# Column halves for the first batch's transform products and three idle products

## The chip, the cores and the metric

The kernel runs on one core of one Trainium2 chip. The metric is the device time of one execution in microseconds; lower is better.

## The reference

Two blocks follow each other. The first is an mLSTM cell over 4 batches, 8 heads, 768 tokens and 40 features a head: a recurrence with a running maximum m for stability.

```
m_new = max(f + m, i);  f_stab = exp(f + m - m_new);  i_stab = exp(i - m_new)
C = f_stab * C + i_stab * outer(v, k);   n = f_stab * n + i_stab * k
y[t] = sigmoid(o) * (C q) / max(|n . q|, 1)
```

Its output, rearranged to x of shape (4, 768, 320), goes into an FNet block: the real part of a two-dimensional Fourier transform over tokens and features, a normalisation, and two dense layers.

```
mixed = real(fft(fft(x, axis=1), axis=2));   u = x + mixed
un = (u - mean(u)) / sqrt(var(u) + 1e-6)
out = u + relu(un @ w_ch1) @ w_ch2           # 320 -> 1280 -> 320
```

## The kernel before

The recurrence is cut into six chunks of 128 tokens a batch. Each chunk needs many small products on TensorE, which all go through the helper `product` (line L587): scores `ps`, outputs `ph` (in the first batch `hb`), and contributions to the state. For batches 1 to 3 they use quadrants of the 128x128 array, so that several run side by side. The maxima of the first batch are spread by `spread_max` (L228, L233).

The Fourier transform uses symmetry. `mix_fold` (L892 to L905) folds tokens and features into sums and differences (`fe`, `fe_odd`). `mix_seq` and `mix_tail` transform over tokens. For the first batch both call `mix_products`, which writes 386 columns (`NK`) for each of three pairs of chunks p, in the order p = 2, 1, 0, and for both parts i (cosine and sine); only part 0 of p = 1 is done otherwise, as two products of 193 columns each (L967, L968, every second column). The results `pz` (128 features) and `pzt` (the last ones, in 64-column tiles, two side by side) are copied by ScalarE to `Z` and `Zt` (L881). `mix_feat` (L1004) then transforms over features: three products of 321 columns for each p into `pu`, and two of 161 columns (`own`) at p = 1. VectorE adds `pu` to x (`mix_add`, L1020) and takes the statistics (L1027, L1028); ScalarE centres (`uc`, L1042), TensorE turns (`put`, L1053), and the dense layers follow: `mlp_in` and the products around it (L1134, L1151, L1217), and the second layer (L1289, L1346). In batches 1 to 3 the transform runs in `mix_products_again` (L958).

While this runs, VectorE and ScalarE also unpack the dense weights from 64-bit words (`Piece`: L465, L467, L473, L480, L483, L487).

`idle_products` (L143) multiplies a tile of zeros into a bank that nobody reads. It is called with three products at the start, before the first gates arrive, and with two more after the last chunk of the first batch.

The order of the work is written out by hand: `at(slot, phase, function)` puts every step into a plan, and `run` issues the steps in order of slot and phase. So every engine executes its instructions in the order in which the plan issued them. Loads and stores are issued from SyncE's queue.

Of the kernel before, what the change touches and what calls it, by code (L numbers as in the profile page):

```python
# [19 lines left out]
L = 128  # L20
# [10 lines left out]
TG = NT // 2  # L31
# [8 lines left out]
NK = HALF + 2  # L40
# [17 lines left out]
def kernel(  # L58
# [15 lines left out]
    nc = tc.nc  # L74
# [19 lines left out]
    def bank(name, shape, n=None):  # L94

        return ps_m.tile(shape, FP, name=name, tag=f"pm{next(turn) if n is None else n}")
# [8 lines left out]
    ds_sb = const.tile([L, TG, 2, NK], FP, name="ds_sb")  # L105
    dd_sb = const.tile([L, 4, DM + 1], FP, name="dd_sb")
    fe = const.tile([L, TG, 2 * PAD], FP, name="fe")
# [29 lines left out]
    EVAC, FILL, MAIN, FILL_PE = range(4)  # L137


    def idle_products(n, rest, at_=None):  # L140
        pw = bank("pi", [L, 2 * L], at_)
        for i in range(n):
            nc.tensor.matmul(pw, rest[:, 0:L], rest, start=True, stop=True, skip_group_check=True)  # L143


    def gates(gp):
# [3 lines left out]
        rest = gp.tile([L, 2 * L], FP, name="rest")  # L150
# [16 lines left out]
        nc.vector.memset(ebias, -896.0 * 2.0**23)  # L167
        nc.gpsimd.memset(qk_bufs[0][:, 0], 0.0)
        nc.scalar.activation(out=warm[:, 0:1], in_=rest[:, 0:1], func=AF.Exp)
        idle_products(3, rest)  # L170
        mlstm_load(0, 0)
        make_identity(nc, ident)
        nc.gpsimd.memset(later_r, 0.0)
# [248 lines left out]
        for c in range(2, NT):  # L422
            for h0 in (0, NP):
                at(3 * c - 1, FILL_PE + 2, spread_max, 0, c, h0)
        at(17, FILL_PE + 2.7, idle_products, 2, rest, 3)
        at(2, FILL + 0.5, columns_late)
        at(2, FILL + 0.6, clear, *gb_bufs)
# [86 lines left out]
    def mlstm_load(b, c):  # L514
        k = chunks[b, c] = Chunk()
        i = b * NT + c
        k.qk = qk_bufs[i % NQ]
        k.C = [states[(c + n if b == 0 else b * NS + 2 * c + n) % len(states)] for n in range(3)]
        for hip in range(2):
            nc.sync.dma_start(out=k.qk[hip * 64:hip * 64 + D], in_=qkT[b, c, hip])  # L520
        kvt = kvp.tile([L, H * (D + D1) + LH - D], FP, name="kvt", tag="kvt")
        nc.sync.dma_start(out=kvt, in_=kv[b, c])
        k.v, k.k = kvt, kvt[:, H * D1:]
        k.v1 = k.v[:, 0:H * D1].rearrange("p (h d) -> p h d", d=D1)
# [394 lines left out]
    def mix_seq(b, p, parts):  # L919


        k = mixes.setdefault(b, Mix())
        if p == TG - 1:
            k.pz = getattr(k, "pz", []) + [bank("pz", [L, NK], MIX[b - 1]["z"][i] if b > 0 else (3, 0)[i]) for i in parts]
        for i in parts:
            if b == 0:
                mix_products(p, k.pz[i], i, slice(0, L))
            else:
                for product in mix_products_again(k, k.pz[i], i, slice(0, L)):
                    product()  # L930

    def mix_tail(b, p):

        k = mixes[b]
        if p == TG - 1:
            k.pzt = bank("pzt", [L, NK], MIX[b - 1]["zt"]) if b > 0 else first_heads_ps[:, 0, 0:NK]
        halves = [k.pzt[i * 64:(i + 1) * 64] for i in range(2)]
        if b == 0:
            for i in range(2):
                mix_products(p, halves[i], i, slice(L, PAD))  # L940
        else:

            a, z = (mix_products_again(k, halves[i], i, slice(L, PAD)) for i in range(2))
            for product in (a[0], z[0], a[1], z[1], a[2], z[2], a[3]):
                product()
# [17 lines left out]
    def mix_products(p, out, i, m):  # L963
        fm = slice(i * PAD + m.start, i * PAD + m.stop)
        kw = dict(stop=(p == 0), skip_group_check=True)
        if i == 0 and p == TG - 2:
            nc.tensor.matmul(out[:, 0:NK:2], fe[:, p, fm], ds_sb[:, p, 0, 0:NK:2], start=False, **kw)  # L967
            nc.tensor.matmul(out[:, 1:NK:2], fe_odd[:, m], ds_sb[:, p, 0, 1:NK:2], start=False, **kw)  # L968
        else:
            nc.tensor.matmul(out, fe[:, p, fm], ds_sb[:, p, i], start=(p == TG - 1), **kw)  # L970

    def mix_seq_out(b, i):
        k = mixes[b]
# [9 lines left out]
    def mix_feat(b, p, part=slice(None)):  # L983

        k = mixes[b]
        m = slice(COL[p], COL[p] + L)
        if part.start in (None, 0):  # L990
            k.pu[p] = bank("pu", [L, DM + 1 + NC], MIX[b - 1]["u"][p] if b > 0 else None)
        pu = k.pu[p]
        if b == 0:
            products = ((pu[:, 0:DM + 1], k.Z[:, 0, m], dd_sb[:, 0]), (pu[:, 0:DM + 1], k.Z[:, 1, m], dd_sb[:, 1]),
                        (pu[:, 0:DM + 1], k.Zt[:, m], dd_sb[:, 2]))
        else:
            products = ((pu[:, 0:NC], k.Z[:, 0, m], dd_sb[:, 0, 0:NC]), (pu[:, NC:DM], k.Z[:, 1, m], dd_sb[:, 1, 1:HALF_D]),
                        (pu[:, 0:DM], k.Zt[:, m], dd_sb[:, 3, 0:DM]))
        if p == TG - 2:
            own = first_heads_ps[:, 1, 0:NC] if b == 0 else pu[:, DM + 1:]  # L1000
            z, zt = (t[:, LAST:LAST + 1].to_broadcast([L, L]) for t in (k.Z[:, 0], k.Zt))
            products += ((own, z, dd_sb[:, 0, 0:NC]), (own, zt, dd_sb[:, 3, 0:NC]))
        for i, (o, z, t) in list(enumerate(products))[part]:
            nc.tensor.matmul(o, z, t, start=(i == 0 or b == 0 and i == 3), stop=(i in (2, 4)), skip_group_check=True)  # L1004

    def mix_add(b, c):

# [74 lines left out]
    def plan_mix(b, s0, x_done, s_feat, s_add, s_turn):  # L1082
# [20 lines left out]
        for p in range(TG):  # L1103
            for i in range(3) if b == 0 and p == TG - 1 else ():
                at(s_feat[p] + i, FILL_PE + 5.1, mix_feat, b, p, slice(i, i + 1))
            if b == 0 and p == TG - 2:
                at(s_feat[p], FILL_PE + 4.06, mix_feat, b, p, slice(0, 3))
                at(s_feat[p] + 1, FILL_PE + 4.95, mix_feat, b, p, slice(3, 5))
            elif b == 0 and p == 0:
                at(s_feat[p], FILL_PE + 4, mix_feat, b, p, slice(0, 2))  # L1110
                at(s_feat[p], FILL_PE + 4.04, mix_feat, b, p, slice(2, 3))
            elif b > 0 or p < TG - 1:
                at(s_feat[p], FILL_PE + 4, mix_feat, b, p)
# [316 lines left out]
    hid.update({(0, r): mlp_p.tile([L, NFF // 2 * TG * L], FP, name=f"h0{r}") for r in range(2)})  # L1430
    gates_pool = ExitStack()
    gates(gates_pool.enter_context(tc.tile_pool(name="gates", bufs=1)))


# [212 lines left out]
```

## Time and profile before

| | |
|---|---|
| median of 3 runs | 383.57 us (379.48 to 384.47) |
| the profiled execution | 382.09 us |
| its span, first to last instruction | 380.2 us |
| TensorE passes, busy | 373.3 us, 4,602 |
| TensorE weight loads, busy | 278.2 us, 4,602 |
| VectorE busy | 280.8 us |
| ScalarE busy | 171.4 us |
| GpSimd busy | 133.9 us |
| mean granted TensorE clock | 0.999 |

The profile calls TensorE's passes PE, its weight loads PEld, VectorE DVE, ScalarE ACT, GpSimd POOL, and SyncE's queue SPq. Durations of passes are modelled and overlap; how fast they follow each other is read from their start times. An fp32 product stands in the profile as two weight loads and two passes. "issue" as the reason of a wait means that the profile shows nothing that the engine waited for. Queue q8 carries instructions, not data.

### The profile page before, as it was taken

Reading aid. Unit: us, or ns where it says so; the run is one execution under the profiler, and the core shown is the slowest. Engines: PE = TensorE matmul, PEld = TensorE weight load, DVE = VectorE, ACT = ScalarE, POOL = GpSimd, SP = SyncE. Lnnn points to the kernel's source line nnn. Section 1 sums busy time; section 2 is a strip of 40 time slices with the busy share of each in tenths; the row PEclk is TensorE's granted clock in tenths of the full one; section 3 lists DMA queues with packets and bytes.
Section 4 is the critical chain, followed back from the end, with each engine's and each line's share of the span. In section 5 each row is a group of like instructions: output and inputs, shape, how many; then the busy total and the mean of one; then the engine's idle time right before and its main releaser. Section 6 shows DMA issues by size and latency. Waiting matters only on the chain.

```text
span 380.2 us, 11433 instructions
## 1 busy us (share of the span) xinstructions
PE 373.3 (98%) x4602; PEld 278.2 (73%) x4602; DVE 280.8 (74%) x662; ACT 171.4 (45%) x501; POOL 133.9 (35%) x240
## 2 busy tenths in 40 slices
PE   8999999999999999999999999999999999999996
PEld 6887655567677777666578999676488996546996
DVE  7788999999998585787964787987745885245552
ACT  4878757756442114764442153854520233544000
POOL 5568433775686124471501424561300000020000
PEclk9999999999999999999999999999999999999999
DMA  7978565999870428460002737300000001000011
GB/s 195 284 219 287 168 184 148 252 241 265 278 207 29 127 66 238 134 174 26 0 3 62 205 99 195 102 3 3 0 2 34 17 20 36 0 0 2 34 36 34
DMA packets 20500, 41.93 MB, mean 110 GB/s; under 512 B 3256, under 2 KB 9744, under 8 KB 20320
## 3 DMA queue, kind: packets, MB, share of 16 engines
q1 hardware_dynamic: 20448, 41.21, 37.5%
q8 instruction: 36, 0.59, 0.7%
q14 instruction: 16, 0.13, 0.1%
HBM read 37.10 MB, written 4.10 MB: 108 GB/s over the span
## 4 chain that ended last, share of the span: by engine, by line
PE 79%; DVE 9%; ACT 2%; issue 1%; SPq 1%; POOL 1%; DMA 0%; DVEq 0%; ACTq 0%; POOLq 0%
PE po L1346 22%; PE pm L1217 19%; PE po L1289 8%; PE pm L1134 7%; PE ph L587 5%; PE pm L1151 4%; PE ps L587 4%; PE pu L1004 3%; PE pz L958 2%; PE put L1053 2%; PE pzt L958 1%; PE hb L587 1%; DVE e L480 1%; DVE stats L1027 1%; DVE e L465 1%
## 5 line engine op out<-in xcount | busy, mean ns | idle before, releaser
L1295 DVE SCALAR_TENSOR_TENSOR x<-po,rstd,x 128x160 f32<-128x160 f32 (+1 forms) x69 | 27.1, 394 | 36.3 <-PE po L1346 33.0
L1223 DVE TENSOR_TENSOR h<-h,pm 128x384 f32<-128x384 f32 x60 | 30.5, 550 | 24.2 <-PE pm L1217 11.8
L583 POOL TENSOR_SCALAR_AFFINE_SELECT W<-W 64x512 f32<-64x512 f32 x36 | 28.1, 780 | 37.8 <-ACT W L556 28.8
L1217 PE MATMUL pm<-uT,w_sb 128*128 128x384 f32 x90 | 37.3, 503 | 0.1
L556 ACT ACTIVATE W<-W,colT 128x64 f32<-128x64 f32 x144 | 36.6, 336 | 1.6 <-DMA W<-M_d 1.6
L710 POOL TENSOR_TENSOR C<-C,decB 128x164 f32<-128x164 f32 x33 | 18.1, 549 | 49.4 <-DVE C L717 45.9
L1289 PE MATMUL po<-w_sb,h 128*128 128x320 f32 x120 | 33.6, 432 | 0.0
L1134 PE MATMUL pm<-uT,w_sb 64*64 64x384 f32 x320 | 32.0, 496 | 0.0
L1077 POOL TENSOR_TENSOR t<-rstd 128x6 f32<-128x6 f32 x12 | 3.7, 311 | 76.1 <-DVE v L1071 75.6
L568 POOL TENSOR_TENSOR qg<-qk,Gb 128x512 f32<-128x512 f32 x21 | 28.1, 1337 | 4.5 <-DMA Gb<-G_d 4.2
L1289 PEld LDWEIGHTS po<-w_sb,h 128*128 128x128 f32 x120 | 22.5, 190 | 8.9
L1151 PE MATMUL pm<-uT,w_sb 128*128 128x384 f32 x80 | 28.4, 496 | 0.0
L1346 PE MATMUL po<-T,S 128*128 128x160 f32 x180 | 27.8, 301 | 0.2 <-DVE x L1295 0.2
L1346 PEld LDWEIGHTS po<-T,S 128*128 128x128 f32 x180 | 25.4, 190 | 1.3 <-DVE x L1295 0.4
L1346 PE MATMUL po<-w_sb,h 128*128 128x160 f32 x180 | 26.3, 300 | 0.0
L1346 PEld LDWEIGHTS po<-w_sb,h 128*128 128x128 f32 x180 | 25.2, 190 | 1.4 <-DVE x L1295 0.3
L1217 PEld LDWEIGHTS pm<-uT,w_sb 128*128 128x128 f32 x90 | 15.7, 189 | 12.1 <-DVE h L1223 4.1
L1272 ACT ACTIVATE h<-h 128x384 f32<-128x384 f32 x45 | 23.1, 520 | 2.9 <-DVE h L1223 2.9
L1134 PEld LDWEIGHTS pm<-uT,w_sb 64*64 64x64 f32 x320 | 11.1, 132 | 15.5 <-issue 13.4
L574 POOL TENSOR_TENSOR vw<-kvt,colT 128x328 f32<-128x328 f32 x23 | 19.6, 852 | 7.0 <-DVE colT L290 2.7
L1151 PEld LDWEIGHTS pm<-uT,w_sb 128*128 128x128 f32 x80 | 14.3, 190 | 10.1 <-issue 1.2
L587 PE MATMUL ps<-qk 40*64 40x64 f32 (+1 forms) x768 | 19.9, 240 | 0.3 <-DVE C L717 0.3
(255 smaller groups left out, 825.2 us busy)
## 6 DMA issues: line engine op xcount, KB each, us to landing
kvt<-in_kv SPq DMA_DIRECT2D x24, 336.0 KB
qk<-in_qkT SPq DMA_DIRECT2D x48, 160.0 KB
raw<-in_w SPq DMA_DIRECT2D x10, 640.0 KB
W<-M_d SPq DMA_DIRECT2D x36, 128.0 KB
so<-in_o SPq DMA_DIRECT2D x24, 160.0 KB
out<-x SPq DMA_DIRECT2D x23, 160.0 KB
Gb<-G_d SPq DMA_DIRECT2D x42, 80.0 KB
ds_sb<-in_dft_s SPq DMA_DIRECT2D x1, 1158.0 KB
```

Source lines behind the costliest of these rows:

```text
L556: nc.scalar.activation(out=k.W[:, h, :], in_=M, func=AF.Exp, scale=-1.0, bias=colT[:, c, 0, b * H + h:b * H + h + 1])
L568: nc.gpsimd.tensor_tensor(out=k.qg[:, :, t], in0=k.qk[:, 0, :, t], in1=k.Gb[:, :, t], op=OP.mult)
L583: nc.gpsimd.affine_select(out=W, in_=W, compare_op=OP.is_ge, fill=0.0, base=base, pattern=[[0, H], [-1 if back else 1, LH]], channel_multi ...
L587: nc.tensor.matmul(out, w, x, start=start, stop=True, skip_group_check=True)
L1134: nc.tensor.matmul(banks[i][half(cols)], w1_rest(n)[half(i), half(cols)], u[half(i)], start=start, stop=not start, skip_group_check=True)
L1151: nc.tensor.matmul(k.pm[i], w1_block(ch, f // 2 * 2 + i), u[2 * ch], start=(ch == 0 and not ahead), stop=(ch == 1 and (ahead or n in (2, 5 ...
L1217: nc.tensor.matmul(bank, w, u, start=start, stop=True, skip_group_check=True)
L1223: nc.vector.tensor_tensor(out=h, in0=h, in1=bank, op=OP.add)
L1272: nc.scalar.activation(out=h, in_=h, func=AF.Relu, scale=-1.0)
L1289: nc.tensor.matmul(k.po[m], hidden(gr, f)[:, i * L:(i + 1) * L], w2_sb[:, f, :], start=(f == 0), stop=(f == NFF - 1))
L1295: nc.vector.scalar_tensor_tensor(out=u, in0=po, scalar=k.rstd[:, c:c + 1], in1=u, op0=OP.mult, op1=OP.add)
L1346: nc.tensor.matmul(po, a[:, f], w[:, f], start=start and f == 0, stop=f == half - 1, skip_group_check=True)
```

## The change

Three kinds of products of the first batch's stretch are issued as two products over halves of their columns, with the same weights: the first three idle products (256 columns become 128 and 128), the ten products of `mix_products` over 386 columns (193 and 193), and the nine products of `mix_feat` over 321 columns (160 and 161). Each half loads its weights again. The flag that clears a bank stays with the first half alone. The two later idle products, the `own` products and all other batches are as before. What follows in TensorE's program stands 88 instructions later.

```diff
+    def columns_of(n, parts):
+        return [slice(i * n // parts, (i + 1) * n // parts) for i in range(parts)]
+
-    def idle_products(n, rest, at_=None):
+    def idle_products(n, rest, at_=None, halves=1):
         pw = bank("pi", [L, 2 * L], at_)
         for i in range(n):
-            nc.tensor.matmul(pw, rest[:, 0:L], rest, start=True, stop=True, skip_group_check=True)
+            for cols in columns_of(2 * L, halves):
+                nc.tensor.matmul(pw[:, cols], rest[:, 0:L], rest[:, cols], start=True, stop=True, skip_group_check=True)
...
-        idle_products(3, rest)
+        idle_products(3, rest, halves=2)
...
-            nc.tensor.matmul(out, fe[:, p, fm], ds_sb[:, p, i], start=(p == TG - 1), **kw)
+            for cols in columns_of(NK, 2):
+                nc.tensor.matmul(out[:, cols], fe[:, p, fm], ds_sb[:, p, i, cols], start=(p == TG - 1 and cols.start == 0), **kw)
...
-            nc.tensor.matmul(o, z, t, start=(i == 0 or b == 0 and i == 3), stop=(i in (2, 4)), skip_group_check=True)
+            for cols in columns_of(o.shape[1], 2 if b == 0 and i < 3 else 1):
+                nc.tensor.matmul(o[:, cols], z, t[:, cols], start=(cols.start == 0 and (i == 0 or b == 0 and i == 3)),
+                                 stop=(i in (2, 4)), skip_group_check=True)
```

## The prediction

> **What bounds the kernel now.** I read the page's busy times first, then the chain of waits in stretches, then TensorE's own timeline around the products that the change cuts, and last the few places where TensorE stands still although nothing holds it.
>
> ```profile
> PE 373.3 (98%) x4602; PEld 278.2 (73%) x4602; DVE 280.8 (74%) x662; ACT 171.4 (45%) x501; POOL 133.9 (35%) x240
> q8 instruction: 36, 0.59, 0.7%
> PE 79%; DVE 9%; ACT 2%; issue 1%; SPq 1%; POOL 1%; DMA 0%; DVEq 0%; ACTq 0%; POOLq 0%
> ```
>
> TensorE is busy for 98% of the span and carries 79% of the chain that ended last. So any time that the change adds to TensorE's program, or takes from it, moves the end, except where another engine holds the chain. The whole chain can therefore not shrink by much: all of TensorE's idle time together is 380.2 - 373.3 = 6.9 us, and some 3 us of that are the last stores after its last pass at 377.1 us. The chain of waits between 36 and 60 us, where most of the cut products run, shows such a place:
>
> ```profile
> 50.27 1.78 DVE w_sb L487
> ...
> 52.08 0.63 DVE e L465
> 52.71 0.40 DVE m L467
> 53.11 0.41 DVE x L1020
> ```
>
> Here VectorE holds the chain, not TensorE: it unpacks weights (L487, L465, L467) and gets to the first add of the transform (L1020) only then. The timeline has TensorE's last two passes for that add (Zt, line L1004) from 51.37 to 52.18; VectorE takes the result up at 53.04, 0.86 us later. What TensorE loses between 42 and 52 us, up to 0.86 us, costs nothing.
>
> **The price of cutting a product.** Each fp32 product appears as two weight loads and two passes (L143: six passes for three products). The change turns 3 + 10 + 9 = 22 products into 44, which is 22 x 4 = 88 instructions. The total number of columns stays the same, so the cost is what a pass costs beyond its columns.
>
> ```profile
> 45.70 0.51 PE L967 MATMUL pz<-ds_sb,fe 128*128 128x193 f32 x2
> 46.04 0.50 PE L968 MATMUL pz<-ds_sb,fe_odd 128*128 128x193 f32 x2
> ```
>
> Columns are start, time, what and count. Two passes of 193 columns take 46.04 - 45.70 = 0.34 us, 170 ns each from start to start. Successive 386-column passes at L970 start 324 ns apart in the same timeline once the first weights are loaded. Two halves then take 340 ns, 16 ns more. These 193-column passes write every second column, and the new ones write neighbouring columns, so 16 ns is my upper bound; the lower is nothing, since the columns are the same. The ten transform products have 20 passes; in the tail products two 64-column tiles run side by side (L970 on hb starts its passes in pairs, at 48.80 and 48.81), so about 15 lie one behind another (10 of the sequence products and 5 steps of the tail's): 0 to 15 x 16 = 0.24 us. The nine feature products (321 columns, passes 270 ns apart) become 160 and 161 columns, and 161-column passes start 136 ns apart: 2 x 136 - 270 = 2 ns, 18 times, 0.04 us. All but the last two or three of these passes lie under VectorE's chain. I take 0.01 us for what gets through and keep 0.28 us for the case that the cover is gone. The weight loads come double, but a load overlaps the pass before it: in L967's two passes each has its own load and they still start 0.17 us apart.
>
> The first three idle products run slowly: passes of 256 columns start 0.43 us apart, and at L233, just after, passes of 128 columns start 0.21 us apart with a load each. Twelve of 0.21 are as long as six of 0.43. What follows them (L273 at 4.10) waits for the last one; I take 0, with 0.1 us either way.
>
> No wait, transfer or queue entry is added; only the last half of a product carries the signal that the whole carried, so ScalarE's copies of Z start when the second half is done. They lie under the same cover.
>
> **The place in the program.** All that follows stands 88 instructions later. That matters only if a position has a price, and one place in the trace looks like it:
>
> ```profile
> 146.86 0.30 PEld L1004 LDWEIGHTS pu<-dd_sb,Z 128*128 128x128 f32 x2
> 147.70 0.32 PEld L1004 LDWEIGHTS pu<-dd_sb,Z 128*128 128x128 f32 x2 [0.54 <-issue]
> 146.86 0.40 PE L1004 MATMUL pu<-dd_sb,Z 128*128 128x161 f32 x1
> 147.69 0.57 PE L1004 MATMUL pu<-dd_sb,Z 128*128 128x161 f32 x3 [0.43 <-issue]
> ```
>
> The second pass of one product has its weights from 147.16 on (loads at 146.86 and 146.97) and the same inputs as the first, yet it starts at 147.69: 0.53 us in which it waits for no engine and no transfer. I read it as an instruction that had not arrived. The page gives queue q8 36 packets of 0.59 MB, 16 KB each; TensorE has 9,204 loads and passes and 93 semaphore instructions, 258 per packet, so q8 brings TensorE's program in blocks of about 256. Narrow windows of the DMA view put one q8 packet into 144.90 to 145.06 and none into 146.2 to 147.2. If the late pass is the first of a block, the others begin every 256 instructions from it, and the block before began at about 144.75 and ran out 2.4 us later. The shortest stretches of 256 instructions, as they stand now (first two) and 88 instructions on (last three):
>
> ```profile
> 144.75:147.70 2.95, 2.52 (x142) 2.37 (x135) 0.72 (x2) 0.61 (x3) 1.34 (x4) 1.00 0.89 226
> 246.10:248.60 2.50, 2.50 (x131) 2.10 (x127) 1.69 (x4) 2.15 (x9) 1.84 (x3) 1.00 0.01 3
> 231.99:235.77 3.78, 3.78 (x141) 3.73 (x133) 2.45 (x8) 1.83 (x5) 1.78 (x3) 1.00 0.47 142
> 169.60:173.52 3.92, 3.92 (x131) 2.74 (x129) 3.18 (x8) 1.42 (x4) 0.82 (x2) 1.00 0.55 144
> 69.70:74.00 4.30, 4.29 (x142) 2.91 (x135) 4.01 (x7) 3.06 (x9) 3.20 (x5) 1.00 0.89 291
> ```
>
> The first number after the window is its length, the first in brackets counts passes, the last but one is the DMA share. Shifted by 88, no block is used up in less than 3.78 us, while the late one needed 2.95. The first took its delay with the DMA engines 89% busy; the one of 2.50 us, with DMA idle, went without. So I expect the 0.53 us to go. The work after it is TensorE's own (L1053, then L1289 without a gap), so the gain passes on. I take -0.5 us, between 0 (it isn't the block) and -0.53.
>
> **The sum.** The profiled execution took 382.09 us, its span 380.2. -0.53 + 0.01 + 0 gives 381.6. The three runs shown have a median of 383.57 and go from 379.48 to 384.47, so the profiled one lies 1.5 below the median, inside their spread of 5 us. 2% of this kernel is 7.7 us, about what a measurement of it can tell from no change. The forecast is no measurable change, with 381.6 us as the time.
>
> **Rivals.**
>
> (1) *The place has no price.* The 0.53 us is something that the trace does not name, and stays. Against it: nothing else there is late. For it: it is a single case, and the 2.50-us block has no gap. Time: 382.09 + 0.01 = 382.1. The Trainium skill speaks for this rival: Runtime: NRT & Kernel Launch, section "Instruction fetch mechanics", says that blocks of 256 instructions are fetched while the previous one executes, and that instruction fetch is hidden because dispatch is slower than the refill. The 0.53 us at 147.2 disagrees with that as far as one case can.
>
> (2) *A new block comes late: slower than before.* Its place is one of the shortest shifted stretches, in or beside the bursts of small products of L587, with 232.0 and 169.6 first. From the start of a block to its packet took 0.3 us in the late case, but up to 3.7 us elsewhere (the next packet starts between 151.35 and 151.50, its block began at 147.70). The packet took 1.28 us and its use came 1.36 us after, so the next block can be there 2.9 to 6.3 us after the start. It decides from 3.78 us on. At the worst end 6.3 - 3.78 = 2.5 us are lost at that one place: 381.6 + 2.5 = 384.1. For over 2%, all four of the shortest (the fourth lasts 4.69 us) would have to be late at the worst end, 2.5 + 2.4 + 2.0 + 1.6 = 8.5 us: 390.1. Against it: all the old blocks over 3 us, some with DMA over 80% busy, show no such gap.
>
> (3) *The cover is gone.* VectorE's chain at 42 to 53 us no longer hides the cut products, because a late Z pushes ScalarE's copies and with them the weight conversions: +0.28 us, 381.9. Against it: 0.86 us of slack.
>
> (4) *The spread itself was late blocks.* If the runs at 383.57 and 384.47 lost several us to blocks that came later than in the profiled execution, the shift would bring all runs near the fastest: 379.48 - 0.5 = 379.0. For it: a spread of 5 us is wide; against it: the profile shows only one such gap. For over 2% the time would have to fall below 0.98 x 383.57 = 375.9, 6.2 us under the profiled execution, more than the 3.9 us that TensorE stands idle before its last pass ends.
>
> **How the numbers follow.** Forecast 0.50, rival 1 0.18, rival 2 0.15 (of which a third at several places together), rival 3 0.05, rival 4 0.12 (of which a good third falls to so far unseen losses that would carry it over 2%). So faster by over 2%: 0.05; slower by over 2%: 0.06, with a little for the unknown; within: 0.89. The range takes the runs' own spread with the bounds on it: 379.48 - 0.5 = 379.0 below, and 384.47 + 0.28 + 0.2 = 385.0 above, which holds rivals 1, 3 and most of 2.
>
> **What would show it.** Right: L1004's passes near 147 us follow each other without an issue gap; 44 more passes and as many loads on TensorE (4,646 each); L970's passes of 193 columns 162 to 170 ns apart; the chain between 50 and 58 us still VectorE's. Wrong: issue gaps in L587's bursts near 74, 173 or 235 us (rival 2), the gap at 147 us still there (rival 1), or the first add of L1020 waiting for pu (rival 3).

## The result and the profile after

The changed kernel took 385.51 us (median of 17 runs, 383.37 to 388.21), the kernel before beside it 381.08 us (17 runs, 379.42 to 384.55). The ratio is 1.0111, with an interval of 1.0087 to 1.0135: 4.4 us slower, where 381.6 us and no measurable change were forecast. It is less than 2%, but it lies outside the predicted range of 379.0 to 385.0 us. Medians here are over all runs, while a ratio leaves out runs more than 1.5% above the fastest of their own kernel.

The page of the profile after, the lines that answer to those shown of before, with the granted clock in 40 slices:

```profile
PE 373.8 (97%) x4646; PEld 282.2 (74%) x4646; DVE 281.3 (73%) x662; ACT 171.1 (45%) x501; POOL 131.8 (34%) x240
PEclk9999999969999999999999999999999999999999
q8 instruction: 36, 0.59, 0.6%
PE 81%; DVE 13%; ACT 2%; issue 2%; POOL 1%; DMA 0%; DVEq 0%; ACTq 0%; POOLq 0%
```

44 passes and 44 loads more, as the change says, and TensorE's busy time has grown by only 0.5 us. So its passes are not what became longer in sum. Two other lines say where to look. The share of "issue" in the chain has gone from 1% to 2%, and one slice of the clock reads 6 instead of 9: near the ninth slice, 77 to 86 us. The waits of TensorE between 58 and 180 us are led by a line that the kernel before does not have (columns: what waited, for what, us in total, times, longest):

```profile
PE ph L591 <- issue: 3.1, 1, 3.1
```

L591 is the `product` helper, L587 before. TensorE's timeline at that place:

```profile
76.73 0.23 PE L591 MATMUL ph<-kvt,W 64*64 64x41 f32 x1
80.02 1.08 PE L591 MATMUL ph<-kvt,W 64*64 64x41 f32 x30 [3.06 <-issue]
81.03 1.65 PE L1158 MATMUL pm<-uT,w_sb 128*128 128x384 f32 x2
```

In the middle of one burst of small products of the same form, TensorE stands still from 76.73 to 80.02 us, 3.28 us from start to start, for no engine and no transfer. Counted along TensorE's program, the stop lies at instruction 2242. The 0.53-us gap of the kernel before lay at 4290, exactly eight times 256 further on. Narrow windows of the DMA view put a q8 packet of 16 KB at 77.30 us; the trace has it on the way for 1.16 us, and TensorE goes on 1.57 us after that. The kernel's windows of 2 us then show what follows (columns: window, its length, busy time and count of PE, PEld, DVE, ACT, POOL, then granted clock, DMA share, GB/s); after first, then the same stretch before:

```profile
76.00:78.00 2.00, 0.96 (x66) 0.84 (x62) 1.97 (x3) 2.00 (x8) 0.98 (x2) 1.00 1.02 290
78.00:80.00 2.00, 0.00 (x0) 0.00 (x0) 1.44 (x3) 0.88 (x4) 1.08 (x2) 0.84 0.84 254
80.00:82.00 2.00, 1.98 (x32) 1.60 (x33) 0.57 (x4) 0.00 (x0) 1.94 (x4) 0.50 0.90 208
82.00:84.00 2.00, 2.00 (x5) 1.09 (x4) 1.97 (x5) 0.58 (x1) 0.98 (x1) 0.50 0.92 213
84.00:86.00 2.00, 2.00 (x4) 1.09 (x4) 1.74 (x3) 0.25 (x1) 0.46 (x1) 0.50 0.99 263
```

```profile
80.00:82.00 2.00, 2.00 (x8) 1.18 (x7) 1.88 (x6) 1.64 (x7) 1.09 (x2) 1.00 1.01 286
82.00:84.00 2.00, 2.00 (x9) 0.93 (x7) 1.92 (x4) 0.07 (x1) 2.00 (x3) 1.00 0.97 212
```

The 2 us from 78 have no pass at all. Then the granted clock is 0.50, and 4 or 5 passes of the first dense layer fit into 2 us instead of 8 or 9. The trace gives the half clock from 79.38 to 86.21 us, 6.83 us; the eight passes of L1158 from 81.03 to 86.26 us start 640 ns apart (the first interval is 798, the last 593) instead of 322 to 323. A busy PE hides this: TensorE counts as 2.00 of 2.00 us busy at half speed.

**Where the 4.4 us come from.** I measure the stretch from the first dense pass (the first of 384 columns) to TensorE's last pass, because what lies ahead of it varies from run to run: in the profiled executions of kernels that do not differ up to there, the full clock began anywhere between 4.6 and 10.8 us, and the transform between 40.5 and 42.7. The stretch grew from 318.42 to 324.08 us, by 5.66: 3.28 us of standstill, 8 passes that took 5.23 instead of 2.68 us at half clock, so 2.55, and 0.53 less because the old gap near 147 us is gone; 0.4 us remain that I do not assign. The stage of the transform, from its first pass to the first dense pass, went from 15.70 to 15.93 us. The profiled execution of after came to its first dense pass 1.98 us sooner (56.40 against 58.38), with the full clock from 4.29 instead of 10.83 us, so its span grew by only 3.7 us; the medians differ by 4.4.

The granted clock of each run tells the same. The profiled run of before, at full clock up to its last passes, has a mean of 0.999; one stretch of 3.41 us at 0.5 takes 0.5 x 3.41 / 381 = 0.0045 from the mean. So I take a mean of 0.9985 or less as at least one stretch at half clock. All 17 runs of the changed kernel are below it, at 0.990 to 0.996. Of the 92 runs of the kernel before beside the experiments, 72 are above, with a median of 380.3 us, and 20 below, with 384.0. So the kernel before runs at half clock for a while too, in about one run of five (what started it in those runs is in no trace); the changed kernel does so in every one.

### The profile page after: what moved, and what is told of

It is laid out like the page before. It is cut to its first block, busy times and chain, and to the rows that moved or that the text cites. A ratio compares the mean times of both kernels' runs of the same rounds, so it can differ in the third digit from the quotient of the medians.

```text
span 383.9 us, 11521 instructions
## 1 busy us (share of the span) xinstructions
PE 373.8 (97%) x4646; PEld 282.2 (74%) x4646; DVE 281.3 (73%) x662; ACT 171.1 (45%) x501; POOL 131.8 (34%) x240
## 4 chain that ended last, share of the span: by engine, by line
PE 81%; DVE 13%; ACT 2%; issue 2%; POOL 1%; DMA 0%; DVEq 0%; ACTq 0%; POOLq 0%
PE po L1353 22%; PE pm L1224 19%; PE po L1296 8%; PE pm L1141 7%; PE ph L591 5%; PE pm L1158 5%; PE ps L591 4%; PE pu L1010 3%; PE pz L962 2%; PE put L1060 2%; DVE e L469 1%; PE pzt L962 1%; DVE e L484 1%; DVE stats L1034 1%; DVE m L487 1%
## 5 line engine op out<-in xcount | busy, mean ns | idle before, releaser
L587 POOL TENSOR_SCALAR_AFFINE_SELECT W<-W 64x512 f32<-64x512 f32 x36 | 27.7, 769 | 38.4 <-ACT W L560 37.2
L1224 PE MATMUL pm<-uT,w_sb 128*128 128x384 f32 x90 | 37.3, 503 | 0.1
L1158 PE MATMUL pm<-uT,w_sb 128*128 128x384 f32 x80 | 30.9, 532 | 0.0
L572 POOL TENSOR_TENSOR qg<-qk,Gb 128x512 f32<-128x512 f32 x21 | 26.9, 1282 | 5.9 <-DMA Gb<-G_d 5.6
L1224 PEld LDWEIGHTS pm<-uT,w_sb 128*128 128x128 f32 x90 | 15.7, 189 | 12.1 <-DVE h L1230 4.1
L1158 PEld LDWEIGHTS pm<-uT,w_sb 128*128 128x128 f32 x80 | 15.5, 205 | 11.3 <-issue 3.9
L591 PE MATMUL ps<-qk 40*64 40x64 f32 (+1 forms) x768 | 19.2, 235 | 0.3 <-DVE C L721 0.3
```

The costliest lines, as they stand in the source:

```text
L572: nc.gpsimd.tensor_tensor(out=k.qg[:, :, t], in0=k.qk[:, 0, :, t], in1=k.Gb[:, :, t], op=OP.mult)
L587: nc.gpsimd.affine_select(out=W, in_=W, compare_op=OP.is_ge, fill=0.0, base=base, pattern=[[0, H], [-1 if back else 1, LH]], channel_multi ...
L591: nc.tensor.matmul(out, w, x, start=start, stop=True, skip_group_check=True)
L1158: nc.tensor.matmul(k.pm[i], w1_block(ch, f // 2 * 2 + i), u[2 * ch], start=(ch == 0 and not ahead), stop=(ch == 1 and (ahead or n in (2, 5 ...
L1224: nc.tensor.matmul(bank, w, u, start=start, stop=True, skip_group_check=True)
```

## Experiments

Tiny products below are 64x64 products over 4 columns of zeros into the bank of the idle products, four instructions each. "Standstill" is the longest time between two starts of TensorE in the block that ends with instruction 2242.

### The place alone: 88 instructions without halves

```diff
+    def filler(n, rest, at_):
+        pw = bank("pi", [L, 2 * L], at_)
+        for i in range(n):
+            hip = j = i % 2
+            r, c = slice(hip * 64, hip * 64 + 64), slice(j * 64, j * 64 + 64)
+            nc.tensor.matmul(pw[c, 0:4], rest[r, 0:64], rest[r, 0:4], start=True, stop=True, skip_group_check=True)
...
         at(17, FILL_PE + 2.7, idle_products, 2, rest, 3)
+        at(17, FILL_PE + 2.71, filler, 22, rest, 3)
```

> The kernel before with 22 small products on zeros (64 rows, 64 weights, 4 columns, nobody reads them) put behind the two idle products near 41 us; no column halves. They are 88 instructions, so everything from the transform on stands where it stands in the changed kernel. Theory P (position: a block of TensorE's program comes late inside a burst of small products near 77 us, and TensorE's clock then drops to half): slower than before by 3 to 5 us, about 385; one gap of 2 to 4 us near 77 to 80 us inside L587's bursts at the same instruction as in the changed kernel, passes of 640 ns behind it, no gap near 147 us. Theory H (the halves themselves cost it: their extra passes and later Z copies): 380.5 to 382.5, the gap near 147 us gone or not, none near 77.

Measured: 385.84 us, ratio 1.0126 (1.0071 to 1.0181). Waits and timeline:

```profile
PE ph L595 <- issue: 3.1, 2, 2.2
```

```profile
77.84 0.23 PE L595 MATMUL ph<-kvt,W 64*64 64x41 f32 x1
80.30 0.67 PE L595 MATMUL ph<-kvt,W 64*64 64x41 f32 x30 [2.24 <-issue]
```

TensorE stops at the same instruction 2242, for 2.46 us, and the clock is 0.5 from 81.63 to 85.04. No product of the kernel is cut here. The stretch from the first dense pass to the last pass is 323.12 us, 4.7 more than before, so the loss is not that of the tiny products, which run ahead of it. A second, shorter stop (1.13 us at 107.71) stands 1,024 instructions behind the first, again a multiple of 256. So the place is enough to make the whole loss.

### Fewer instructions: only the ten products of the transform in halves

```diff
-        idle_products(3, rest, halves=2)
+        idle_products(3, rest)
...
-            for cols in columns_of(o.shape[1], 2 if b == 0 and i < 3 else 1):
+            for cols in columns_of(o.shape[1], 1):
```

> Only the ten transform products in halves: 40 instructions. Theory P: by the positions in the trace of before, a block then begins near 76.6 us and is used up in 2.5 us, so the next one comes late at the 2,202nd instruction or so, by 0.4 to 5 us, and with over 3 us the clock drops as well: 382 to 389, with the gap near 79 us and not near 77. Theory H: 40/88 of 4.4 us, 383, without a gap.

Measured: 385.85 us, ratio 1.0112 (1.0062 to 1.0163). What follows stands 40 instructions later. TensorE stands still for 2.57 us at 75.67, once more at instruction 2242 (the expectation had counted on about 2,202 and 79 us), and the clock is 0.5 from 76.89 to 83.72. The runs split: three of ten at 381.8 to 382.4 us with the clock at 1.000, the other seven at 383.4 to 388.2 with 0.986 to 0.996. So a smaller shift is as bad, but not in every run.

### The halves with the place given back: 256 instructions

A shift by a whole block of 256 leaves every block at the work that it had before. First with 42 tiny products more beside the two idle products of slot 17:

```diff
         at(17, FILL_PE + 2.7, idle_products, 2, rest, 3)
+        at(17, FILL_PE + 2.71, filler, 42, rest, 3)
```

> The changed kernel with 42 such small products behind the two idle products: 168 instructions, with the 88 of the halves 256, one whole block, so the block ends fall on the same instructions as before the change from the transform on. Theory P: no gap near 77 us and no passes at 640 ns; the gap of half a us near 147 us back; the small products take 1.5 to 2.7 us of which 0.9 is hidden, so 381 to 383.5. Theory H: 385.5 or more.

Measured: 383.94 us, ratio 1.0112 (1.0058 to 1.0167). This did not settle it by its time: behind the tiny products the clock is 0.5 from 42.44 to 45.85 us, in the transform, and all six runs have a clock of 0.996 or less. But no standstill is left near 77 us, and the stretch from the first dense pass is 317.96 us. So I moved the tiny products to the start, where TensorE waits for the gates:

```diff
-        idle_products(3, rest, halves=2)
+        filler(42, rest, idle_products(3, rest, halves=2))
```

> The changed kernel with 42 more tiny products (168 instructions) right behind the three idle products at the start, where TensorE waits for the gates, so that all behind the transform stands 256 instructions later, a whole block: the blocks begin at the same work as in the kernel before. Theory P (the place in the program is what costs; the halves by themselves cost 0 to 0.3 us): no standstill near 76 us, clock 1.0 after the start, the stretch from the first dense pass to the last pass of TensorE as before (318.4 us, give or take 0.6), the gap near 147 us comes back, and the median is within 0.4% of before. Rival H (the halves themselves cost): the stretch or the stage of the transform is 3 us or more longer and the ratio is 1.008 or more again.

Measured: 385.24 us, ratio 1.0113 (1.0067 to 1.0158), so the expectation of the time failed; the reason stands at the very start of the timeline, and the windows near the place show the rest:

```profile
4.09 4.65 PE L155 MATMUL pi<-rest 64*64 64x4 f32 x84
```

```profile
78.00:80.00 2.00, 2.00 (x49) 0.98 (x48) 1.97 (x4) 0.90 (x4) 2.00 (x3) 1.00 0.85 233
80.00:82.00 2.00, 1.73 (x109) 1.61 (x106) 2.00 (x4) 1.90 (x6) 1.85 (x3) 1.00 1.08 289
82.00:84.00 2.00, 2.00 (x27) 1.29 (x20) 1.97 (x4) 1.82 (x8) 0.14 (x2) 1.00 0.91 280
```

The 84 tiny passes took 4.65 us, and the first gate product came after them, at 8.67 us, so TensorE was not as idle there as I had thought. That start, 4.57 us later than in the kernel before (4.10), is enough for the 3.8 us by which the median is longer. Behind it everything is as before the change: the burst that ends the block runs through at full clock, five of six runs have a clock of 1.000, the transform stage takes 15.69 us (15.70 before) and the stretch behind it 317.93 (318.42). All 22 halved products are in this kernel, and their stop is gone with the place. The stage of the transform hides part of their price here, because VectorE holds it up for 0.8 us as in the kernel before. The two kernels below with all 22 halves, few loads or none, and no such hold of VectorE took 14.99 us for it, against 14.89 with the same few loads and no halves. So the halves' own price is about 0.1 us, within the 0.28 of the prediction, and the place makes the loss. The gap near 147 us did not come back, though the blocks lie as before there: its packet started 0.19 us ahead of the block instead of 0.30 after, so that gap is a matter of tenths from run to run.

### Another place: 120 instructions

```diff
+        at(17, FILL_PE + 2.71, filler, 30, rest, 3)
```

> The kernel before with 30 tiny products (120 instructions) at the two idle products of slot 17 and no halves. By the times of the kernel before, blocks would then be used up in 2.2 us from 69.2, in 2.4 us from 98.7, in 3.5 us from 131.4 and in 2.0 us from 163.4 us. Theory P: TensorE stands still at the ends of the first two of these, near 71 and 101 us, for 1 to 3.5 us each, where neither the kernel before nor the one with 88 instructions stands still so long, and perhaps at the others; nothing at 77 us; the granted clock is 0.5 after the longer ones; 383 to 389 us. Rival H or F (the tiny products cost by their number): as with 22 of them, 0.5 us more at most, and no standstill at the two places.

Measured: 387.99 us, ratio 1.0102 (1.001 to 1.0194); three of four runs at 387.5 to 392.7 us with the clock at 0.982 to 0.995, one at 382.25 with 1.000.

```profile
77.14 0.39 PE L595 MATMUL ps<-vw,kvt 64*40 64x41 f32 x18
80.43 0.43 PE L595 MATMUL ps<-vw,kvt 64*40 64x41 f32 x11 [2.89 <-issue]
```

That is slow as the place would have it, but with the standstill where I had been sure of none, and, but for a shorter one at 169.8 us, none where I had put it. The burst at 69 us, used up in 2.3 us, lost next to nothing, because its packet started 0.52 us ahead of the block. The one that stopped TensorE for 3.09 us was a block that lasted 7 us, and its packet started 7.59 us after the block. Therefore the time in which a block is used up does not say whether the next one is late. What matters is when its packet starts.

### What the packet waits for: less data

The stop lies where the DMA engines are 84% to 102% busy (a window counts a packet whole where it starts, so a share can pass 100%). So the next kernels take loads away. First the second piece of second-layer weights alone (640 KB, issued at 73.47 us in the changed kernel):

```diff
+            if self is w2_pieces[1]:
+                self.raw = w2_pieces[0].raw
+                return
             self.raw = cp.tile([L, n], mybir.dt.int64, name="raw", tag="raw")
```

> The changed kernel without one load: the 640 KB of weights that its trace shows issued at 73.47 us (the second piece of the second layer's weights) are not loaded, and the piece before is unpacked in their place, so that part of the output is computed with other weights; all engines execute the same instructions. Theory P with the late block queued behind this load: the gap near 77 us shrinks to under 1 us, no passes at 640 ns, 380 to 382.5. If the block is late for another reason: gap of 3 us as in the changed kernel, 384.5 to 386. Theory H: 385 to 386.

Measured: 382.15 us, ratio 1.0058 (1.0017 to 1.0099); standstill 1.91 us. Six of ten runs have the full clock, with a median of 381.4, the other four 384.4. A second stop, of 1.02 us, stands at 105.94 us. The same with three such loads (near 66, 73 and 81 us):

```diff
+            if self in w2_pieces[0:3]:
+                self.raw = w1_pieces[4].raw
+                return
```

> The changed kernel without three weight loads of 640 KB each (the first three pieces of the second layer's weights, issued near 66, 73 and 81 us); the piece before is unpacked in their place, so that part of the output is computed with other weights; all engines execute the same instructions. If the block near 77 us is late behind data: the packet starts within 3 us of its block's start, the gap is under 1 us, the clock doesn't drop, 380 to 382. If data don't matter: gap of 3 us, 385.

Measured: 383.75 us, ratio 1.0082 (1.0052 to 1.0113); standstill 2.46 us. That is not better than with one load, against what a queue of data alone would do; a reason would be that the other loads move up into the room, which I did not follow up. So I left out the chunk's own loads too, in the changed kernel and, for the comparison, in the kernel before:

```diff
-        for hip in range(2):
+        skip = i in (9, 10, 11)
+        for hip in range(0 if skip else 2):
             nc.sync.dma_start(out=k.qk[hip * 64:hip * 64 + D], in_=qkT[b, c, hip])
...
+        if not skip:
+            chunks["kvt"] = kvp.tile([L, H * (D + D1) + LH - D], FP, name="kvt", tag="kvt")
+            nc.sync.dma_start(out=chunks["kvt"], in_=kv[b, c])
+        kvt = chunks["kvt"]
```

> The changed kernel without the loads that are issued from 65.8 to 85 us of three pieces of second-layer weights, of kvt and of qk (older data stand in for them), so that the output is not that of the reference; W, so and Gb are still loaded. Theory Q (the packet that brings a block of TensorE's program queues behind the kernel's own data): with less than half of the bytes left between 66 and 82 us, the packet of the block that begins near 72.2 us starts less than 2 us after it (5.05 us in the changed kernel), no standstill is left at instruction 2242 of TensorE's program, the granted clock stays at 1.0 there, and the median is within 0.4% of that of the next kernel, which leaves out the same loads before the change. Rival R (the packet is late by itself, whatever the data do): it starts 4 to 5 us after the block's beginning again, the standstill is 2 to 3 us, and the median is 3 to 5 us above that of the next kernel.

> The kernel before without the same loads as in the run above (older data stand in). Both theories: within 2 us of the kernel before, 378.5 to 381 us, clock 1.0; it is there as the other half of the comparison. If the loads themselves cost TensorE time between 66 and 90 us, it is faster than before by that much.

Measured: 382.44 us, ratio 1.0028 (0.9984 to 1.0071), against 380.02 us and 0.9966 (0.9928 to 1.0004): 0.6% between the two, half of what the change costs with all loads. Four of ten runs of the first have the full clock (380.1 us), all ten of the second. In the profiled run the packet was no earlier for it: it started 4.78 us after the block, with the standstill 2.46 us, in windows like these:

```profile
72.00:74.00 2.00, 2.00 (x45) 0.89 (x44) 1.97 (x4) 0.81 (x4) 2.00 (x3) 1.00 0.32 98
74.00:76.00 2.00, 1.72 (x94) 1.49 (x85) 2.00 (x4) 1.90 (x6) 1.85 (x3) 1.00 0.41 146
76.00:78.00 2.00, 0.01 (x1) 0.00 (x0) 1.97 (x4) 1.94 (x9) 0.15 (x2) 1.00 0.32 104
```

A DMA share of 0.3 to 0.4 and a packet as late as with 0.9: data in front of it are not the whole story. Two more kernels were made for this question alone. One leaves out nearly all data there, the other moves the block against the work and leaves the data alone:

```diff
+            if b * NT + c in (10, 11):
+                continue
             nc.sync.dma_start(out=k.W[i * LH:(i + 1) * LH],
...
-            for hip in range(2):
+            for hip in range(0 if i in (9, 10, 11) else 2):
                 h = slice(b * H + hip * NP, b * H + (hip + 1) * NP)
```

> The changed kernel without the loads of three pieces of second-layer weights and, of three chunks, without those of kvt, qk, so, Gb and (of two of them) W, all of which fell between 66 and 85 us; older data stand in, so that the output is not that of the reference. Theory Q (what holds the packet up is data in front of it): with nothing left to move between about 72 and 78 us, the packet of the block that begins near 71 to 72 us starts within 1 us of the block's beginning, no standstill is left at instruction 2242, clock 1.0, 379 to 381 us. Rival W (it is asked for only when TensorE comes to a certain place in the block, behind the wait and the slow passes with which this block begins): it starts again when the burst near 74.5 us is under way, some 3 to 5 us after the block's beginning, and TensorE stands still for 1 to 2.5 us with DMA idle.

```diff
+        at(17, FILL_PE + 2.71, filler, 4, rest, 3)
```

> The changed kernel with four more tiny products (16 instructions) at slot 17: the block in question begins 16 instructions earlier in the work, with about 40 instead of 24 instructions of slow passes ahead of its dense burst, near 69.7 instead of 72.2 us. Theory Q: its packet, asked for 2.5 us earlier, starts that much earlier, so that the standstill near 76.7 us goes or shrinks from 3.3 us to 1 us at most. Rival W with the place more than 40 instructions into the block: the packet starts at the same work as before (76 to 77.5 us) and the standstill stays 2.5 to 3.5 us; W with the place at 25 to 40 instructions: as Q.

Measured without the loads: 381.61 us, ratio 1.0026 (0.9986 to 1.0066); six of ten runs have the full clock. The DMA view between 72.3 and 75.05 us has no packet, and the next window has one:

```profile
DMA packets 0, 0.00 MB, mean 0 GB/s; under 512 B 0, under 2 KB 0, under 8 KB 0
```

```profile
q8 instruction: 1, 0.02, 5.7%
```

```profile
74.03 0.68 PE L601 MATMUL ph<-C,qg 40*64 40x41 f32 x32
...
76.27 0.28 PE L601 MATMUL ph<-kvt,W 64*64 64x41 f32 x2
77.70 0.77 PE L601 MATMUL ph<-kvt,W 64*64 64x41 f32 x20 [1.16 <-issue]
```

All DMA engines are idle for nearly 3 us, and still the packet starts only at 75.08, 3.62 us after its block began (71.45) and 1.08 us after the first small product of the burst (74.00). TensorE stands still for 1.38 us, with no data in the packet's way. Two later blocks of the same trace, at 86.81 and 93.04 us, with the DMA engines as idle, had their packets after 0.74 and 0.73 us. So I read it as asked for late. With four more tiny products the block begins 2 us sooner, at 70.16 us, and the packet does not: 77.43, standstill 3.34 us; three of four runs at 386.4 to 386.9 us, one, with the clock at 1.000, at 380.58 us. This trace has one more stop, of 1.78 us at 106.60, again 1,024 instructions further on:

```profile
PE ps L599 <- issue: 3.1, 1, 3.1
PE pm L1166 <- issue: 1.3, 1, 1.3
```

All nine kernels with this stop, from their traces:

| kernel | block begins | first small product of the burst | packet starts | after the block's beginning | after the small product | DMA share in between | standstill |
|---|---|---|---|---|---|---|---|
| after | 72.25 | 74.40 | 77.30 | 5.05 | 2.90 | 0.98 | 3.28 |
| shift by 88 | 73.35 | 75.50 | 77.84 | 4.50 | 2.34 | 1.02 | 2.46 |
| shift by 104 | 70.16 | 74.71 | 77.43 | 7.27 | 2.72 | 1.03 | 3.34 |
| shift by 120 | 70.39 | 75.18 | 77.98 | 7.59 | 2.80 | 0.97 | 3.09 |
| ten products in halves | 73.18 | 73.18 | 75.56 | 2.38 | 2.38 | 1.03 | 2.57 |
| one load left out | 71.95 | 74.28 | 75.31 | 3.36 | 1.03 | 0.66 | 1.91 |
| three loads left out | 72.16 | 74.29 | 76.33 | 4.18 | 2.04 | 0.85 | 2.46 |
| few loads | 70.98 | 73.46 | 75.76 | 4.78 | 2.30 | 0.42 | 2.46 |
| no loads | 71.45 | 74.00 | 75.08 | 3.62 | 1.08 | 0.00 | 1.38 |

From the block's beginning the packet takes 2.4 to 7.6 us, without order; from the first small product 1.0 to 2.9 us. In eight of the nine, that product stands behind a semaphore instruction of TensorE and up to 56 instructions of dense passes (384 columns, 0.32 us a pass on the whole array). With ten products in halves the block begins inside the burst. The reading that fits both is that the request comes when TensorE's program has got past the dense passes, not when the block begins; it is argued from these times and was not tried by itself. Data in front of the packet would then add up to 1.8 us (2.90 against 1.08). Two rows do not fit a mean share alone: few loads, with 2.30 us at 0.42, and one load left out, with 1.03 us at 0.66, no more than without loads; which of the DMA engines carries the packet is not in the trace. Which instruction makes the request stays open too: it was not tried to move that wait.

### More data, and shifts elsewhere

Three dummy loads of 400 KB in the kernel before, near 80 us:

```diff
+    for n, t in enumerate(("T2", "T3", "T4")):
+        at(37, FILL + 0.5 + n / 100, lambda t=t: nc.sync.dma_start(out=w2x[t].rearrange("p f m -> p (f m)"), in_=spare))
```

> The kernel before with three extra loads of 400 KB from a table into tiles that are written over later, issued near 80 us; TensorE's program is that of before, instruction for instruction. If blocks of TensorE's program are late because their packets stand behind data: the packet that came at 82.2 us comes 1 to 5 us later and a gap that nothing explains appears at the 2,498th instruction (near 87 us), 0.5 to 3 us long, perhaps with the clock dropping; 382 to 387. If position alone decides and data don't matter: no such gap, 381 to 382.5 (waits for data that the extra loads push back would show as waits for a DMA).

Measured: 384.91 us, ratio 1.0101 (1.0063 to 1.014). As many microseconds, but the profiled run has another cause, at 91.1 us:

```profile
93.42 0.69 PE L587 MATMUL ps<-qk 40*64 40x64 f32 x32 [2.09 <-DVE C L717]
```

It waits for VectorE, which in the chain of waits stands behind a weight load on the way from 85.39 us for 6.23 us (raw). The packets of the blocks were later (3.39 us after the block near 75 us, 0.88 in the kernel before), but none too late. So this run shows no late block, and it says little on the question. Seven of its ten runs are below 0.9985, but the profiled one is one of the other three: what held those seven up is in no trace.

One idle product fewer in slot 17, four instructions the other way:

```diff
-        at(17, FILL_PE + 2.7, idle_products, 2, rest, 3)
+        at(17, FILL_PE + 2.7, idle_products, 1, rest, 3)
```

> The kernel before with one later idle product instead of two: 4 instructions less, so every block from there on begins 4 instructions later in the work. Theory P: by the trace of before the block in front of the late pass at 147.7 us then lasts 3.2 us instead of 2.4 to 2.95, so its gap of 0.53 us goes, and the other short blocks (84 us: 2.8 us, 246 us: 2.5 us) stay in time: 317.8 to 318.4 us from the first dense layer's start to the last pass, the whole 379 to 381. If the gap isn't the block's, it stays and nothing changes.

Measured: 380.81 us, ratio 0.9995 (0.9966 to 1.0024): no difference that can be told. The profiled run has late blocks all the same: at 83.57 us for 3.41 us, and, against the expectation, still at the place of the old gap, now at 150.4 us, for 1.23 us from start to start where the kernel before had 0.72. Three of its twelve runs are below 0.9985, a share like that of the kernel before.

The transform of the last batch in halves (23 products), behind all dense bursts:

```diff
+            for part in (slice(first, cut, step), slice(cut, NK, step)) if k is mixes.get(B - 1) else (cols,):
+                nc.tensor.matmul(out[:, part], f, ds_sb[:, p, i, part], start=(n == 0 and part.start == first),
+                                 stop=(n == len(products) - 1), skip_group_check=True)
```

> The kernel before with 23 products of the last batch's transform (near 285 to 305 us) in column halves instead of the first batch's: as many extra passes, but nothing stands elsewhere before 285 us, and behind it a block lasts over 15 us. Theory P (position): no late block in the bursts near 77 us; from the start of the first dense layer to the last pass 318 to 319.5 us as before (318.4), the whole 380.5 to 382.5. Theory H (the halves cost it): 4 us more, about 385.

Measured: 383.3 us, ratio 1.0061 (1.002 to 1.0102), eight of ten runs at full clock. Up to 285 us this is the program of before, yet the stretch from the first dense pass is 323.10 us instead of the 318 to 319.5 expected, and three blocks are late in the profiled run, with starts 1.66, 0.97 and 1.00 us apart, at 83.75, 91.77 and 146.60 us:

```profile
PE ph L587 <- issue: 1.4, 1, 1.4
PE ps L587 <- issue: 0.8, 1, 0.8
PE pu L1009 <- issue: 0.7, 1, 0.7
```

So how late a block is changes from run to run in the same program. At the end the halves do cost, without any late block behind them: from the block at 264 us to TensorE's last pass 114.5 us instead of 112.8. Most of these products have 193 columns already. Their passes start 172 ns apart in the median, those of the halves of 96 and 97 columns 110 and 113, so two halves take 51 ns more. So the near-zero price of a cut was measured for 386 and 321 columns in two, and does not hold for 193.

## Why the prediction was wrong

**What held.** The count of instructions and passes (4,646) was right. So was the price of the cuts: passes of 193 columns start 163 and 167 ns apart, 330 ns for two against 324 to 329 for one of 386, 6 ns at most where 16 was the bound, and the whole transform stage lost 0.23 us or less. VectorE still holds the chain in that stage:

```profile
48.06 0.84 DVE w_sb L491
...
48.92 1.54 DVE e L469
50.47 0.67 DVE m L471
51.13 0.41 DVE x L1027
```

The reading of the 0.53-us gap as a late block was right, and the gap went with the shift, as forecast: in the timeline after, the passes from 151.12 (L1010) follow each other without a break. The stops of all runs at distances of 256 instructions from it, with a q8 packet landing 1.3 to 1.7 us ahead of each, bear out that reading of q8.

**The step that failed** is the one from the shortest shifted stretches to "no block is late". It gave the fourth shortest as 4.69 us (in the trace of before, the block from 74.0 to 78.7 us), and set against it the 2.95 us of the one late block. That measures how long a block lasts, and the runs show that this alone does not decide: a block of 2.3 us was in time in the run with 120 instructions, one of 7 us was 3.1 us late. In the changed kernel the block at 74.0 (now from 72.25 to 76.73, 4.48 us) had its dense passes first and its burst last. The packet of the next came only in the burst; counted from there it had 2.33 us (74.40 to 76.73), not 4.48, against 2.90 to its start, 1.16 on the way and 1.57 to its use. That the packet was late is measured; why it was asked for then, and by which instruction, stays open.

**Rival 2 was what happened**, and it was mis-sized twice. Its bound on the way from block to packet was 3.7 us, by the largest value that one row of before showed; it measured 5.05 here and up to 7.59. By the rival's own formula 6.3 - 4.69 = 1.6 us would have been lost at this place; it was 3.28. And it had no term for what comes behind a standstill: 6.83 us at half clock, 2.55 us more. It put 232.0 and 169.6 first, the shortest stretches; neither stopped TensorE in the profiled run of after. DMA was 47% and 55% busy there in the table of before, against 89% at 69.7 to 74.0, just ahead of the block in question, a number in the same rows that the ranking did not use.

The Trainium skill, Runtime: NRT & Kernel Launch, section "Instruction fetch mechanics", calls the refill hidden, since dispatch is slower than the fetch. Standstills of 1.38 to 3.34 us at block boundaries in nine kernels disagree, for bursts of small products. The same section of the Trainium skill says that the sequencer drives its own queue, by markers at block boundaries; a request in program order agrees with that, but in the run without loads the packet started 3.62 us behind the boundary, with the DMA engines idle for most of that time, so a request at the boundary itself does not.

**Rivals 3 and 4.** The cover was not gone, and the price is no larger without it. The kernel with ten products in halves had no such stop of VectorE in its profiled run and took 14.97 us for the transform stage; the two with no cut and no stop (one idle product fewer; halves in the last batch) took 14.89 and 14.90, and the two with all 22 halves and no stop 14.99. With the stop it is 15.70 before and 15.93 after. Rival 4 had a point that I undervalued: part of the spread of the kernel before is half clock, 20 of 92 runs with 3.7 us more, and late blocks come and go in its program, as the run with halves in the last batch shows. The shift did not cure these runs but made all runs like them.

**The measurement.** The prediction took 2%, 7.7 us, as about what a measurement can tell from no change. With 17 runs of each kernel the interval of the ratio is 0.0048 wide, 1.8 us, so a change of 4.4 us is clear of the noise.

## What to carry to other kernels

Where a burst of small products follows a few dense passes, any edit that changes the number of TensorE instructions ahead of it can stop TensorE there, as four different shifts did here; look in the timeline for a stop put down to "issue" inside a burst, and count instructions modulo 256 from one known stop. A change that only moves the program should be compared with the same shift made of empty products, before its own merit is judged. Read the granted clock of the windows behind each standstill: the busy share stays at its maximum while the passes take twice as long; none of the kernels here that do the whole work beat the one before.

## What was not expected

- The price of a standstill nearly doubles behind it. In all nine kernels of the table, a stop of 1.38 to 3.34 us inside a burst went with 3.41 or 6.83 us at a granted clock of 0.5, which began during the stop or at most 1.4 us after it. A stop of 1.66 us (83.75 us, halves in the last batch), one of 1.78 us (106.60 us, shift by 104) and a wait of 2.09 us (91.3 us, with the dummy loads) had none, so the length of a stop alone does not decide. The Trainium skill, TensorE: Matmul & The Clock Gate, Part 1, gives windows of 3.41 us and names an idle window of about that length as what lowers the clock. The lengths agree; but here a stop of 1.38 us, 0.4 of such a window, went with half clock, inside a burst of small products. Whether these products count as idle is not shown.
- VectorE's weight conversion depends on when GpSimd works. In ten of the 16 traces one of its steps in the transform took 1.44 to 1.89 us, each time beside the same GpSimd step (L568 of the kernel before); in the other six none took over 0.83. The last step of one piece (L487) took 0.83 us with GpSimd idle (halves in the last batch) and 1.77 us where GpSimd's L568 ran from 49.66 to 51.36 us (before). In after the next step met it, L469 with 1.54 us instead of 0.49, beside L572 from 48.84 to 50.11. GpSimd starts when Gb has landed. So VectorE's hold on the chain in the transform, 0.8 us, comes and goes from run to run, and the prediction's 0.86 us of cover were such a meeting.
